# A list schedule with a price for the SBUF port of VectorE and GpSimd, in a kernel of attention and two feed-forward layers

## The chip, the cores and the metric

One core of a Trainium2 chip. The metric is the device time of one execution in microseconds, as a median of runs; the profile is of one execution.

## The reference

Attention for 2 batches x 8 heads x 768 positions x 64 dimensions, in which a query sees only keys of its own bucket (the signs of six projections), and then two feed-forward layers over 1536 tokens of width 512 with a hidden width of 2048:

```python
mask = q_bucket[:, :, :, None] == k_bucket[:, :, None, :]
scores = np.where(mask, scale * np.matmul(q, k.transpose(0, 1, 3, 2)), -1e9)
x = softmax(scores) @ v            # as (1536, 512)
h = np.maximum(x @ w_in, 0.0)
x = h * h @ w_out
h = x @ w2_in
out = (h * np.tanh(np.log1p(np.exp(h)))) @ w2_out
```

The four weight matrices come as 64-bit floats, which the kernel reads as pairs of 32-bit words and converts itself.

## The kernel before, in words

**Attention** (to about 224 us) is written out by hand in the order of its steps. Its last act on GpSimd (POOL) is `finish` (L564): it adds and scales the tiles `hi` and `rb` into `xf`, the input of the first layer. While it runs, five weight pieces are converted (`early`), so the feed-forward part begins with four up pieces and one down piece of its first group of weights.

**The feed-forward layers** go by a planner. Every 32-bit operand of a product is a pair of rounded parts, high and low; a product is three matmuls (`three`, L949 to L951): high x high, high x low, low x high. The hidden width of each layer is cut into four groups (`i` = 0 to 3 for the first layer, 4 to 7 for the second), each with 4 up pieces `wi` and 4 down pieces `wo`. The tokens form three blocks of 512. For each group the up products are:

- `classic`: block 0, four products of 12 matmuls (u = 0 to 7 in units of six matmuls);
- `seven`, twice: blocks 1 and 2 by seven half-size products in place of eight (Strassen's way), 6 matmuls each. They read sums of x blocks (`B11`, `B21`, `T1` to `T4`, `B22`, made once per layer by `blocks_x`) and sums of weights (`a`, `s`, made per group by `blocks_w`), and VectorE (DVE) puts the seven results together from PSUM (`add`, on DVE alone).

`activate` (L965) then takes relu and square, or mish, and splits the result into `gh` and `gl`. Down products (`half_down`, 24 per group, 6 matmuls each, numbered d) sum over the four pieces into four accumulators `acc` of PSUM; `collect` adds these to `tot`, by DVE (the first group of a layer is copied by ScalarE, ACT).

**The planner.** Each step is a `Task` with a due time, a cost for each engine that could do it, and what it comes after. `Plan.run` (L100) repeats: of all tasks whose inputs are planned, for each engine that would end it first, take the one that starts earliest, then the one due earliest; it is emitted on that engine's queue and the engine is taken to be busy for the cost. All engines work in order, so the plan is the order of their queues. It knows nothing of waits for memory that earlier tiles used. Its helpers:

- `both` (L765): a sum or difference of two tiles, on DVE or POOL; L770 is its instruction;
- `copy` (L774): a rounded copy, on ACT (L779) or POOL (L781);
- `parts`: a `copy` for the high part, a `both` for the low one;
- `convert` (L825): a load of a weight piece into one of two staging buffers, then on DVE magnitude (L842), bound (L845), move (L848), low (L851) and sign (L854), then `parts`;
- `when_up(u)` and `when_down(d)` give due times; `convert` and the x blocks are due some units before their products.

The table of activation functions for mish is loaded by a task of ACT at 100 of the plan's microseconds.

```python
    cost = {V: (n + 70) / 960, GP: 2.3e-3 * n + 0.12}       # both
    cost = {A: 0.833e-3 * n + 0.11, GP: 0.95e-3 * n + 0.2}  # copy
    plan.run({V: 2.5, A: 2.5, GP: 7.7, SP: 0.0, PE: 0.0})
```

Of the kernel before, what the change touches and what calls it, by code (L numbers as in the profile page):

```python
# [9 lines left out]
F32 = mybir.dt.float32  # L10
# [3 lines left out]
AF = mybir.ActivationFunctionType  # L14
ALU = mybir.AluOpType
# [4 lines left out]
EXP_SET, MISH_SET = TABLES.index("exp_and_others"), TABLES.index("mish")  # L20
# [17 lines left out]
class Buffer:  # L38


    def __init__(self, ring, size, make):
        self.ring, self.size, self.make = ring, size, make
        self.tile, self.left, self.end = None, 0, 0.0


class Task:

    def __init__(self, due, cost, emit, after, uses, lag):
        self.due, self.cost, self.emit, self.after, self.uses, self.lag = due, cost, emit, after, uses, lag
        self.end = self.behind = None  # L50


class Plan:
# [12 lines left out]
            self.rings.setdefault(ring, []).append(b)  # L66
        return b

    def task(self, due, cost, emit, after=(), uses=(), lag=0.0):
        t = Task(due, cost, emit, list(after), list(uses), lag)  # L70
        for b in t.uses:
            b.left += 1
        self.tasks.append(t)
        return t

    def given(self, end):
        t = Task(0.0, {}, None, [], [], 0.0)
        t.end = end
        return t

# [17 lines left out]
        return at  # L98

    def run(self, free):  # L100
        waiting = list(self.tasks)
        while waiting:
            best = {}
            for n, t in enumerate(waiting[:400]):
                at = self.ready(t)
                if at is None:
                    continue
                ends = {e: max(free[e], at) + c for e, c in t.cost.items()}
                first = min(ends.values())
                for e, c in t.cost.items():  # L110
                    if ends[e] <= first:
                        start = max(free[e], at)
                        key = (start, t.due, n)
                        if e not in best or key < best[e][0]:
                            best[e] = key, t
            e = min(best, key=lambda e: best[e][0])
            (start, _, _), t = best[e]
            for b in t.uses:
                if b.tile is None:
                    b.tile = b.make()  # L120
                    self.rings[b.ring].append(b)
            t.emit(e)
            free[e] = start + t.cost[e]
            t.end = free[e] + (t.lag or self.HOP)
            for b in t.uses:
                b.left -= 1
                b.end = max(b.end, t.end)
            waiting.remove(t)
# [3 lines left out]
def lsh_attention_relu2_mish_kernel(ctx, tc, qT, kT, vP, proj, w_in, w_out, w2_in, w2_out, out):  # L132
# [27 lines left out]
    def load_table(k):  # L160
        loaded.append(k)
        nc.scalar.add_instruction(
            mybir.InstLoadActFuncSet(act_func_set_id=k, name=nc.get_next_instruction_name(), ins=[], outs=[])
        )
# [581 lines left out]


    tmp = ctx.enter_context(tc.tile_pool(name="tmp", bufs=NTMP, reuse_waits="tile"))
    gp = ctx.enter_context(tc.tile_pool(name="gp", bufs=NGP, reuse_waits="tile"))
    wb = ctx.enter_context(tc.tile_pool(name="wb", bufs=1, reuse_waits="tile"))  # L750
    sw = ctx.enter_context(tc.tile_pool(name="sw", bufs=NS, reuse_waits="tile"))
    sf = ctx.enter_context(tc.tile_pool(name="sf", bufs=1, reuse_waits="tile"))
    pacc = ctx.enter_context(tc.tile_pool(name="pacc", bufs=4, reuse_waits="tile", space=PSUM))
    psh = ctx.enter_context(tc.tile_pool(name="psh", bufs=4, reuse_waits="tile", space=PSUM))
    wpools[1] = wb
# [8 lines left out]

    def both(due, out, a, b, n, after, uses, op=ALU.subtract, on=(V, GP)):  # L765

        cost = {V: (n + 70) / 960, GP: 2.3e-3 * n + 0.12}

        def emit(e):
            e.tensor_tensor(out(), a(), b(), op)  # L770

        return plan.task(due, {e: cost[e] for e in on}, emit, after, uses)

    def copy(due, out, a, n, after, uses, on=(A, GP), func=AF.Copy):  # L774
        cost = {A: 0.833e-3 * n + 0.11, GP: 0.95e-3 * n + 0.2}

        def emit(e):
            if e is A:
                e.activation(out(), a(), func)  # L779
            else:  # L780
                e.tensor_scalar(out(), a(), 1.0, 0.0, ALU.mult, ALU.add)  # L781

        return plan.task(due, {e: cost[e] for e in on}, emit, after, uses)

    def parts(due, high, low, a, n, after, uses):

# [5 lines left out]
    PERIOD, HALVES = 2 * FC + 2 * 7, 2 * FC * NBLK  # L792
    UNIT = 6 * 0.2265

    def when_up(u):
        return UNIT * (u + max(0.0, HALVES * (u - LAG) / PERIOD))

    def when_down(d):
        i, n = divmod(d, HALVES)
        u = LAG + PERIOD * d / HALVES  # L800
        if i == G - 1:
            u = min(u, G * PERIOD + 2 + 0.01 * n)
        return when_up(u) + (UNIT * n * 0.001)

    SA, SB = 2, 1
    ORDERS = {0: (0, 1, 2, 3), SB: (0, 1, 3, 2), SA: (0, 1, 2, 3)}
# [4 lines left out]


    W, Wd = {}, {}
    order = [None]

    def place(nm, i, f):
        W[nm, i, f] = plan.buffer("w" + nm, 5, lambda: new_place(nm, i, f))
# [7 lines left out]
    def convert(k, due):  # L825
        i, nm, src, f = pieces[k]
        if k in staged:
            s, load = plan.buffer("stg", 2, tile=staged.pop(k)), [plan.given(0.0)]
        else:
            s = tile_of(stg, [P, 512], I64, "stg", 2)  # L830
            load = [plan.task(due, {SP: 0.7}, lambda e: e.dma_start(out=s.tile, in_=src[i % G, :, f * 512:(f + 1) * 512]), [], [s], 4.5)]
        m = tile_of(stg, [P, 512], F32, "cv", 2)
        w = place(nm, i, f)

        def word(n):
            return s.tile.bitcast(U32).rearrange("p (n t) -> p n t", t=2)[:, :, n]

        def mu():
            return m.tile.bitcast(U32)

        def magnitude(e):
            e.tensor_scalar(mu(), word(1), 0x7FFFFFFF, None, ALU.bitwise_and)  # L842

        def bound(e):
            e.tensor_scalar(m.tile, m.tile, F64_LOW, F64_HIGH, ALU.max, ALU.min)  # L845

        def move(e):
            e.tensor_scalar(mu(), mu(), 3, 0x3FFFFFF8, ALU.logical_shift_left, ALU.bitwise_and)  # L848

        def low(e):  # L850
            e.scalar_tensor_tensor(mu(), word(0), 29, mu(), ALU.logical_shift_right, ALU.bitwise_or)  # L851

        def sign(e):
            e.scalar_tensor_tensor(mu(), word(1), 0xC0000000, mu(), ALU.bitwise_and, ALU.bitwise_or)  # L854

        after = load + [order[0]] * (order[0] is not None)
        for emit, cost in ((magnitude, 0.35), (bound, 0.35), (move, 0.35), (low, 0.61), (sign, 0.61)):
            after = [plan.task(due, {V: cost}, emit, after, [s, m])]
        order[0] = after[0]
        Wd[nm, i, f] = parts(due, lambda: w.tile[:, 0], lambda: w.tile[:, 1], lambda: m.tile, 512, after, [m, w])  # L860
        for t, prev in zip(Wd[nm, i, f][:1], last_w.get(nm, [])):
            t.after.append(prev)
        last_w[nm] = Wd[nm, i, f]

    last_w = {}
# [93 lines left out]
    def bank():  # L959
        return tile_of(psh, [P, TB], F32, "h", 4)  # L960

    ready, gb = {}, {}
    table = plan.task(100.0, {A: 2.0}, lambda e: load_table(MISH_SET), [plan.given(100.0)])

    def activate(i, blk, f, due, h, after, t=None):  # L965

        uses = [h] if t is None else []
        t = temporary() if t is None else t
        a = (lambda: t.tile) if not uses else (lambda: h.tile)
        o = copy(due, lambda: t.tile, a, TB, after + [table] * (i >= G), [t] + uses, (A,), AF.Relu if i < G else AF.Mish)  # L970
        due += 2
        if i < G:
            cost = {A: 0.54, V: 0.61, GP: 1.3}

            def square(e):
                if e is A:
                    e.activation(t.tile, t.tile, AF.Square)
                else:
                    e.tensor_tensor(t.tile, t.tile, t.tile, ALU.mult)

            o = plan.task(due, cost, square, [o], [t])
        if (i, blk, f) == (2 * G - 1, SA, FC - 1):
            gh, gl = (tile_of(tmp, [P, TB], F32R, "t", NTMP) for _ in range(2))
        else:
            gh, gl = (tile_of(gp, [P, TB], F32R, tag, NGP) for tag in ("gh", "gl"))
        gb[i, blk, f] = gh, gl
        r = copy(due, lambda: gh.tile, lambda: t.tile, TB, [o], [t, gh])
        ready[i, blk, f] = [r, both(due, lambda: gl.tile, lambda: t.tile, lambda: b32(gh.tile), TB, [r], [t, gh, gl])]
# [135 lines left out]
    for i in range(2 * G):  # L1124
        if i == G:
            X[1, "x"] = tile_of(act, [P, 2, PPB, TB], F32R, "xs", 1)
            for c in range(PPB):
                x_parts((1, "x"), c, when_up(G * PERIOD) - 4, lambda c=c: tot[0, 0].tile[:, c, :], [totd[0, c]], [tot[0, 0]])
            blocks_x(1, [tot[0, blk] for blk in range(NBLK)], dict(totd))
        if i:  # L1130
            for nm in "io":
# [60 lines left out]
```

## Time and profile before

| what | value |
|---|---|
| median of 3 runs | 777.0 us (775.19 to 779.73) |
| the profiled execution | 778.28 us, of which the span is 776.3 |
| TensorE (PE) busy | 739.3 us, 95% |
| VectorE (DVE) busy | 668.8 us, 86% |
| ScalarE (ACT) busy | 400.6 us, 52% |
| GpSimd (POOL) busy | 377.5 us, 49% |
| the chain that ended last | PE 55%, DVE 37%, issue 4%, ACT 2% |
| mean granted clock of TensorE | 0.98 |

Matmuls overlap, each one counted from its start to its end, so a TensorE that starts them at half its pace looks busy as well. The pace is read from the starts of neighbours, and the work of a stretch from its number of matmuls.

### The profile page before, as it was taken

The page shows a single profiled execution, that of the slowest core. Times are in us where ns is not written, and L with a number is a line of the kernel's source. Part 1 is how long each engine was busy: PE and PEld are TensorE (multiplying, and loading weights), DVE is VectorE, ACT ScalarE, POOL GpSimd, SP SyncE. Part 2 cuts the span into 40 slices and gives each one's busy share as a digit, 9 for nine tenths or more (in the row PEclk, how much of TensorE's full clock was granted, in tenths as well). Part 3 has the DMA queues.
Part 4 walks back from the last instruction along what each step waited for, and adds up shares of the span by engine and source line. Part 5 has one row for each costly group of instructions (what it writes and reads, how often), then busy time and mean ns, then how long its engine had stood idle before and what let it go on. Part 6 is the DMA issues. An engine that isn't in the chain of part 4 may idle for free.

```text
span 776.3 us, 10726 instructions
## 1 busy us (share of the span) xinstructions
PE 739.3 (95%) x3658; PEld 627.3 (81%) x3658; DVE 668.8 (86%) x1060; ACT 400.6 (52%) x729; POOL 377.5 (49%) x400
## 2 busy tenths in 40 slices
PE   8999999999996799899998998989999899999998
PEld 5999999999984488678887887867878688878887
DVE  8989998999959999999699799999989966995543
ACT  6989888988974354453343334434343322231320
POOL 8685967584228625145255136554644342561100
PEclk9999999999998899999999999998999999999999
DMA  6778777875310123221112121200222211120012
GB/s 183 210 187 215 185 170 203 214 176 133 97 51 0 30 79 109 84 97 64 56 54 82 54 79 58 82 28 27 82 82 81 82 55 54 55 77 4 1 55 108
DMA packets 29102, 72.70 MB, mean 94 GB/s; under 512 B 5064, under 2 KB 10536, under 8 KB 29048
## 3 DMA queue, kind: packets, MB, share of 16 engines
q1 hardware_dynamic: 28824, 71.88, 32.6%
q8 instruction: 29, 0.48, 0.3%
q14 instruction: 25, 0.20, 0.1%
q10 hardware_dynamic: 224, 0.13, 0.1%
HBM read 46.14 MB, written 3.19 MB: 64 GB/s over the span
## 4 chain that ended last, share of the span: by engine, by line
PE 55%; DVE 37%; issue 4%; ACT 2%; DMA 1%; POOL 1%; SPq 0%; POOLq 0%; ACTq 0%; DVEq 0%
PE acc L517 8%; PE s L462 8%; PE pT L488 8%; DVE t L770 7%; PE acc L949 6%; PE acc L951 6%; PE acc L950 6%; PE h L949 4%; PE h L951 4%; PE h L950 4%; DVE gl L770 4%; DVE a L770 3%; DVE cv L854 3%; DVE cv L851 3%; DVE cv L845 3%
## 5 line engine op out<-in xcount | busy, mean ns | idle before, releaser
L505 DVE TENSOR_TENSOR pl<-pT,ph 128x768 fp32r<-128x768 f32 x96 | 91.7, 956 | 16.7 <-ACT ph L501 10.5
L779 ACT ACTIVATE t<-t 128x512 f32<-128x512 f32 (+1 forms) x65 | 41.0, 632 | 119.6 <-DVE t L770 118.9
L478 ACT ACTIVATE e<-e,nm 128x768 f32<-128x768 f32 x96 | 89.8, 935 | 8.1 <-DVE e L469 7.9
L469 DVE TENSOR_SCALAR_CACHE_REDUCE e<-s 128x768 f32<-128x768 f32 x96 | 90.8, 946 | 0.9 <-PE s L462 0.8
L949 PE MATMUL acc<-gh,wo 128*128 128x512 f32 x192 | 76.6, 399 | 9.5 <-DVE tot L770 4.0
L501 ACT ACTIVATE ph<-pT 128x768 fp32r<-128x768 f32 x96 | 77.7, 809 | 12.2 <-PE pT L490 7.0
L770 DVE TENSOR_TENSOR t<-t,h 128x512 f32<-128x512 f32 x112 | 74.7, 678 | 9.5 <-PE h L951 9.5
L770 DVE TENSOR_TENSOR gl<-t,gh 128x512 fp32r<-128x512 f32 x79 | 62.0, 787 | 23.8 <-ACT gh L779 22.6
L488 PE MATMUL pT<-ident,e 128*128 128x128 f32 x576 | 78.9, 273 | 0.3 <-DVE e L469 0.2
L949 PE MATMUL acc<-wo,gh 128*128 128x512 f32 (+1 forms) x191 | 74.1, 388 | 5.0 <-DVE tot L770 5.0
L951 PE MATMUL acc<-gh,wo 128*128 128x512 f32 x192 | 75.8, 395 | 1.1 <-DVE wo L770 1.1
L950 PE MATMUL acc<-gl,wo 128*128 128x512 f32 x192 | 75.9, 395 | 0.0
L951 PE MATMUL acc<-wo,gl 128*128 128x512 f32 (+1 forms) x191 | 74.0, 388 | 0.6 <-DVE gl L770 0.6
L950 PE MATMUL acc<-wo,gh 128*128 128x512 f32 (+1 forms) x191 | 73.7, 386 | 0.0
L488 PEld LDWEIGHTS pT<-ident,e 128*128 128x128 f32 x576 | 67.4, 140 | 6.2 <-DVE e L469 1.6
L779 ACT ACTIVATE t<-h 128x512 f32<-128x512 f32 x48 | 28.4, 591 | 82.2 <-PE h L951 79.8
L770 POOL TENSOR_TENSOR a<-wi 128x256 f32<-128x256 f32 x44 | 41.3, 944 | 50.5 <-DVE wi L770 49.3
L770 DVE TENSOR_TENSOR tot<-tot,acc 128x512 f32<-128x512 f32 (+1 forms) x73 | 47.0, 674 | 19.0 <-PE acc L951 19.0
L770 POOL TENSOR_TENSOR s<-a,s 128x256 fp32r<-128x256 f32 x55 | 51.5, 947 | 2.8 <-ACT s L779 1.8
L949 PEld LDWEIGHTS acc<-gh,wo 128*128 128x128 f32 x192 | 36.7, 191 | 19.5 <-issue 8.2
L462 PE MATMUL s<-KA,QA 128*128 128x384 f32 x192 | 50.0, 342 | 0.4 <-DVE q_r L389 0.2
L462 PE MATMUL s<-KB,QB 128*128 128x384 f32 x192 | 49.3, 338 | 0.9 <-DVE QB L357 0.9
(191 smaller groups left out, 1926.4 us busy)
## 6 DMA issues: line engine op xcount, KB each, us to landing
stg<-in_w_in_dram SPq DMA_DIRECT2D x32, 512.0 KB
stg<-in_w_out_dram SPq DMA_DIRECT2D x32, 512.0 KB
KA<-kh SPq DMA_DIRECT2D x28, 192.0 KB
v_r<-in_vP_dram SPq DMA_DIRECT2D x8, 384.0 KB
rb<-rd SPq DMA_DIRECT2D x32, 96.0 KB
out_dram<-tot SPq DMA_DIRECT2D x11, 256.0 KB
q_r<-in_qT_dram SPq DMA_DIRECT2D x7, 384.0 KB
k_r<-in_kT_dram SPq DMA_DIRECT2D x7, 384.0 KB
```

Source lines behind the costliest of these rows:

```text
L462: nc.tensor.matmul(ps[:, o], a[:, q0:q0 + P], b[:, H2 * h:H2 * h + H2], start=n == 0, stop=n == 1)
L469: nc.vector.tensor_scalar(e.rearrange("p (h s) -> p h s", s=H2), x, MASKED, None, ALU.min, ALU.min, accum_out=nm)
L478: nc.scalar.activation(e, e, AF.Exp, bias=nm, scale=-1.0, accum_out=ssums[p, half][:, c:c + 1])
L488: nc.tensor.transpose(ps[:, c * P:(c + 1) * P], e[:, c * P:(c + 1) * P], ident)
L501: nc.scalar.activation(ph, v, AF.Copy)
L505: nc.vector.tensor_tensor(pl, v, b32(ph), ALU.subtract)
L517: nc.tensor.matmul(accs[g], w, phl[g][k // KT][:, c, :], start=k == 0, stop=k == 2 * KT - 1)
L770: e.tensor_tensor(out(), a(), b(), op)
L779: e.activation(out(), a(), func)
L949: PE.matmul(out, a[k][0], b[k][0], start=first and k == 0, stop=False)
L950: PE.matmul(out, a[k][0], b[k][1], start=False, stop=False)
L951: PE.matmul(out, a[k][1], b[k][0], start=False, stop=final and k == n - 1)
```

## The change

1. A task has a `port`: the engines on which it holds the SBUF port that DVE and POOL share. The planner starts such a task only when the port is free, and holds the port to its end. `both` holds it on either engine where POOL is a choice; the conversions' steps hold it on DVE, the square on DVE and POOL. Sums from PSUM, on DVE alone, don't. The costs of `both` and `copy` change a little.
2. `copy` is for ACT alone. The magnitude of a first-layer piece goes to ACT, as an activation (absolute value).
3. Due times: the first block's eight down products (d < 8) are due right behind the first four `classic` ones, and the up products from u = 8 on are put off by up to eight units; the rule for the last group of the first layer is written anew.
4. The table load comes behind the last magnitude and the first layer's last up product.
5. The pools `sw` and `sf` (tiles `s` and `a`) are allocated ahead of `gp` and `wb`. The magnitudes of successive pieces are no longer chained; the first step of a piece comes behind the high part of the piece before it.

```diff
+    def task(self, due, cost, emit, after=(), uses=(), lag=0.0, port=()):
...
     def run(self, free):
-        waiting = list(self.tasks)
+        waiting, port = list(self.tasks), 0.0
...
-                ends = {e: max(free[e], at) + c for e, c in t.cost.items()}
-                first = min(ends.values())
+                starts = {e: max(free[e], at, port if e in t.port else 0.0) for e in t.cost}
+                first = min(starts[e] + c for e, c in t.cost.items())
                 for e, c in t.cost.items():
-                    if ends[e] <= first:
-                        start = max(free[e], at)
-                        key = (start, t.due, n)
+                    if starts[e] + c <= first:
+                        key = (starts[e], t.due, n)
...
             free[e] = start + t.cost[e]
+            if e in t.port:
+                port = free[e]
...
     tmp = ctx.enter_context(tc.tile_pool(name="tmp", bufs=NTMP, reuse_waits="tile"))
+    sw = ctx.enter_context(tc.tile_pool(name="sw", bufs=NS, reuse_waits="tile"))
+    sf = ctx.enter_context(tc.tile_pool(name="sf", bufs=1, reuse_waits="tile"))
     gp = ctx.enter_context(tc.tile_pool(name="gp", bufs=NGP, reuse_waits="tile"))
     wb = ctx.enter_context(tc.tile_pool(name="wb", bufs=1, reuse_waits="tile"))
-    sw = ctx.enter_context(tc.tile_pool(name="sw", bufs=NS, reuse_waits="tile"))
-    sf = ctx.enter_context(tc.tile_pool(name="sf", bufs=1, reuse_waits="tile"))
...
-        cost = {V: (n + 70) / 960, GP: 2.3e-3 * n + 0.12}
+        cost = {V: (n + 66) / 960, GP: 2.5e-3 * n + 0.1}
...
-        return plan.task(due, {e: cost[e] for e in on}, emit, after, uses)
+        return plan.task(due, {e: cost[e] for e in on}, emit, after, uses, port=on if GP in on else ())
...
-    def copy(due, out, a, n, after, uses, on=(A, GP), func=AF.Copy):
-        cost = {A: 0.833e-3 * n + 0.11, GP: 0.95e-3 * n + 0.2}
+    def copy(due, out, a, n, after, uses, on=(A,), func=AF.Copy):
+        cost = {A: 0.833e-3 * n + 0.11, GP: 0.9e-3 * n + 0.2}
...
+    AHEAD = 8
+
     def when_up(u):
-        return UNIT * (u + max(0.0, HALVES * (u - LAG) / PERIOD))
+        return UNIT * (u + max(AHEAD * min(1.0, max(0.0, u - 7.5)), HALVES * (u - LAG) / PERIOD))
 
     def when_down(d):
-        i, n = divmod(d, HALVES)
-        u = LAG + PERIOD * d / HALVES
-        if i == G - 1:
-            u = min(u, G * PERIOD + 2 + 0.01 * n)
-        return when_up(u) + (UNIT * n * 0.001)
+        if d < AHEAD:
+            return UNIT * (8.01 + d)
+        if (G - 1) * HALVES <= d < G * HALVES:
+            return min(when_up(LAG + PERIOD * d / HALVES), when_up(G * PERIOD + 2) + 0.001 * d)
+        return when_up(LAG + PERIOD * d / HALVES)
...
         def magnitude(e):
-            e.tensor_scalar(mu(), word(1), 0x7FFFFFFF, None, ALU.bitwise_and)
+            if e is A:
+                e.activation(m.tile, s.tile.bitcast(F32).rearrange("p (n t) -> p n t", t=2)[:, :, 1], AF.Abs)
+            else:
+                e.tensor_scalar(mu(), word(1), 0x7FFFFFFF, None, ALU.bitwise_and)
...
-        after = load + [order[0]] * (order[0] is not None)
-        for emit, cost in ((magnitude, 0.35), (bound, 0.35), (move, 0.35), (low, 0.61), (sign, 0.61)):
-            after = [plan.task(due, {V: cost}, emit, after, [s, m])]
-        order[0] = after[0]
+        after = load + last_w.get(nm, [])[:1]
+        first = (A, 0.57) if i < G else (V, 0.35)
+        for emit, e, cost in ((magnitude, *first), (bound, V, 0.35), (move, V, 0.35), (low, V, 0.61), (sign, V, 0.61)):
+            after = [plan.task(due, {e: cost}, emit, after, [s, m], port=(V,))]
+            if e is A:
+                magnitudes.extend(after)
...
-        for t, prev in zip(Wd[nm, i, f][:1], last_w.get(nm, [])):
-            t.after.append(prev)
...
-    table = plan.task(100.0, {A: 2.0}, lambda e: load_table(MISH_SET), [plan.given(100.0)])
...
-            o = plan.task(due, cost, square, [o], [t])
+            o = plan.task(due, cost, square, [o], [t], port=(V, GP))
...
+            table.append(plan.task(when_up(G * PERIOD), {A: 1.4}, lambda e: load_table(MISH_SET), magnitudes + list(up[-1:])))
```

## Rows read from the trace of the kernel before

**Rows 1.** Windows by stage: us, each engine's busy us (instructions), TensorE's clock, DMA share, GB/s

```profile
224.60:300.00 75.40, 62.74 (x247) 48.25 (x246) 67.32 (x98) 35.11 (x66) 44.49 (x44) 0.91 0.17 50
300.00:515.00 215.00, 205.95 (x891) 169.04 (x891) 196.39 (x310) 89.38 (x154) 91.14 (x103) 0.98 0.21 69
515.00:540.00 25.00, 21.62 (x79) 15.68 (x78) 24.90 (x33) 11.50 (x21) 15.50 (x14) 0.86 0.12 40
540.00:700.00 160.00, 154.33 (x672) 126.70 (x671) 140.53 (x219) 51.39 (x92) 75.87 (x83) 0.99 0.22 70
...
224.60:776.30 551.70, 517.77 (x2217) 420.50 (x2215) 465.36 (x712) 202.45 (x356) 232.92 (x250) 0.97 0.19 62
```

**Rows 2.** Timeline of TensorE: neighbours at full pace, and behind a wait

```profile
244.07 0.63 PE L949 MATMUL h<-T,s 128*128 128x512 f32 x1
244.50 0.63 PE L950 MATMUL h<-T,s 128*128 128x512 f32 x1
...
406.72 0.39 PE L950 MATMUL h<-B,wi 128*128 128x512 f32 x1
406.95 0.39 PE L951 MATMUL h<-B,wi 128*128 128x512 f32 x1
```

**Rows 3.** Waits of TensorE from 224.6 us: in total, times, longest

```profile
PE acc L949 <- DVE tot L770: 9.0, 4, 3.2
PE h L950 <- DVE B L770: 5.7, 3, 3.1
PE h L950 <- DVE T L770: 4.2, 3, 3.3
```

**Rows 4.** Timeline of DVE beside an idle POOL: start us, duration us

```profile
258.60 0.68 DVE L854 SCALAR_TENSOR_TENSOR cv<-stg,cv 128x512 uint32<-128x512 uint32 x1
259.20 0.41 DVE L770 TENSOR_TENSOR a<-wi 128x256 f32<-128x256 f32 x1
259.54 0.42 DVE L842 TENSOR_SCALAR cv<-stg 128x512 uint32<-128x512 uint32 x1
259.88 1.21 DVE L770 TENSOR_TENSOR T<-t,T 128x512 fp32r<-128x512 f32 x1
```

**Rows 5.** Timelines of DVE and of POOL where both work

```profile
240.65 1.21 DVE L770 TENSOR_TENSOR gl<-t,gh 128x512 fp32r<-128x512 f32 x1
241.78 1.21 DVE L770 TENSOR_TENSOR B<-xf,B 128x512 fp32r<-128x512 f32 x1
...
241.27 1.17 POOL L770 TENSOR_TENSOR s<-a,s 128x256 fp32r<-128x256 f32 x1
```

**Rows 6.** L770 alone in the window; POOL's 256-wide groups of it (busy, mean ns, idle)

```profile
224.60:776.30 551.70, 295.01 (x410) 180.27 (x170) 0.97 0.19 62
...
L770 POOL TENSOR_TENSOR s<-a,s 128x256 fp32r<-128x256 f32 x55 | 51.5, 947 | 2.8 <-ACT s L779 1.8
L770 POOL TENSOR_TENSOR a<-wi 128x256 f32<-128x256 f32 x44 | 41.3, 944 | 50.5 <-DVE wi L770 49.3 <-DVE s L770 0.4
L770 POOL TENSOR_TENSOR a<-a,a 128x256 f32<-128x256 f32 x38 | 40.2, 1057 | 14.0 <-DVE a L770 13.2
```

**Rows 7.** Waits of DVE between 224.6 and 300 us

```profile
DVE a L770 <- POOL hi L568: 5.9, 1, 5.9
```

**Rows 8.** Timelines of ACT and TensorE at two losses; in brackets, idle before

```profile
322.84 0.63 ACT L779 ACTIVATE wo<-cv 128x512 fp32r<-128x512 f32 x1 [2.52 <-DVE cv L854]
...
325.44 0.47 PE L949 MATMUL acc<-gh,wo 128*128 128x512 f32 x1 [3.02 <-ACT tot L779]
...
416.13 0.47 PE L949 MATMUL acc<-gh,wo 128*128 128x512 f32 x1 [2.00 <-DVE tot L770]
```

**Rows 9.** Timeline of DVE at the boundary of the layers

```profile
516.12 5.32 DVE L770 TENSOR_TENSOR B<-tot,B 128x512 fp32r<-128x512 f32 x4
```

**Rows 10.** Timeline of ACT at the table load

```profile
347.94 1.28 ACT L162 ACT_TABLE_LOAD   x1
349.23 0.42 ACT L779 ACTIVATE s<-a 128x256 fp32r<-128x256 f32 x1
```

More of the change, by code (lines that the diff above doesn't have):

```diff
@@ L46, with __init__ @@
 class Task:
-    def __init__(self, due, cost, emit, after, uses, lag):
-        self.due, self.cost, self.emit, self.after, self.uses, self.lag = due, cost, emit, after, uses, lag
+    def __init__(self, due, cost, emit, after, uses, lag, port):
+        self.due, self.cost, self.emit, self.after, self.uses, self.lag, self.port = due, cost, emit, after, uses, lag, port
         self.end = self.behind = None
@@ L67, in buffer @@
         return b
-    def task(self, due, cost, emit, after=(), uses=(), lag=0.0):
-        t = Task(due, cost, emit, list(after), list(uses), lag)
+    def task(self, due, cost, emit, after=(), uses=(), lag=0.0, port=()):
+        t = Task(due, cost, emit, list(after), list(uses), lag, port)
         for b in t.uses:
@@ L76, in given @@
     def given(self, end):
-        t = Task(0.0, {}, None, [], [], 0.0)
+        t = Task(0.0, {}, None, [], [], 0.0, ())
         t.end = end
@@ L781, in emit @@
                 e.tensor_scalar(out(), a(), 1.0, 0.0, ALU.mult, ALU.add)
-        return plan.task(due, {e: cost[e] for e in on}, emit, after, uses)
+        return plan.task(due, {e: cost[e] for e in on}, emit, after, uses, port=(GP,))
     def parts(due, high, low, a, n, after, uses):
@@ L813, in lsh_attention_relu2_mish_kernel @@
     W, Wd = {}, {}
-    order = [None]
+    magnitudes = []
     def place(nm, i, f):
@@ L960, in bank @@
         return tile_of(psh, [P, TB], F32, "h", 4)
-    ready, gb = {}, {}
-    table = plan.task(100.0, {A: 2.0}, lambda e: load_table(MISH_SET), [plan.given(100.0)])
+    ready, gb, table = {}, {}, []
     def activate(i, blk, f, due, h, after, t=None):
@@ L969, in activate @@
         a = (lambda: t.tile) if not uses else (lambda: h.tile)
-        o = copy(due, lambda: t.tile, a, TB, after + [table] * (i >= G), [t] + uses, (A,), AF.Relu if i < G else AF.Mish)
+        o = copy(due, lambda: t.tile, a, TB, after + table, [t] + uses, (A,), AF.Relu if i < G else AF.Mish)
         due += 2
```

## The prediction

> **What bounds it now.** I read the windows by stage first. From 224.6 us on TensorE has one stream of products left: 2217 matmuls, 24 of them half as wide [rows 1]. At full clock one starts every 0.2265 us [rows 2], so they need 2193 x 0.2265 + 24 x 0.12 (my estimate for the half width) = 500 us. They take from 224.6 to 773, 548: some 48 us are lost, and nothing but these can be won. The same division, window by window, says where: 247 matmuls in 224.6 to 300 leave 19.5 us; 891 in 300 to 515 leave 13.2; 79 in 515 to 540 leave 7.1; 672 in 540 to 700 leave 7.8; behind 700 nothing is lost [rows 1]. The reader is to see VectorE (DVE) beside that: busy 88 to 99% of the windows where TensorE loses time, and 36 of the last 76 us, where it loses none.
>
> TensorE's waits name the same engine: DVE's `tot` adds, which free the accumulators, and the x blocks B and T [rows 3]. After a wait the clock adds to it: behind a wait for B that ends at 243.05, the longest with 3.1 us [rows 3], matmuls start every 0.43 us [rows 2], about the lower of the two levels (1.2 and 2.4 GHz), in a window with a mean granted clock of 0.91 [rows 1].
>
> Then why DVE is late. Beside an idle GpSimd (POOL) a 512-wide instruction with two SBUF inputs takes 0.60 us from start to start, a 256-wide one 0.34, a `tensor_scalar` 0.34 [rows 4]. Beside a busy POOL the 512-wide one takes 1.13, and POOL's 256-wide one 1.17 [rows 5], where the plan's price for it is 0.71 (its groups have means of 0.94 to 1.06 [rows 6]). The two hold each other up almost fully, and the plan before knows nothing of it: it prices each engine as if the other stood still.
>
> **The change, part by part.** *The port in the plan.* L770 issues 410 instructions on DVE and 170 on POOL; 137 of POOL's are 256 wide [rows 6]. At the prices of [rows 4] DVE's own 410 cost at most 410 x 0.60 = 246 us (some are narrower), the 59 pieces not converted early 59 x (3 x 0.34 + 2 x 0.60) = 131, the seven others of its 712 instructions 4: 381, where DVE was busy 465 [rows 1]. So POOL stretched DVE by 84 or more. If DVE did all of POOL's 170, that is 137 x 0.34 + 33 x 0.60 = 66. The magnitudes of the 27 pieces of the first layer that were not converted early leave DVE: minus 9. DVE then has 438 us against TensorE's 500, 88%, even if POOL does nothing. In the new plan POOL still wins a 256-wide task while DVE adds from PSUM, which takes no port there.
>
> *Rounded parts and magnitudes on ScalarE (ACT).* At most 80 POOL copies (250 instructions less the 170 [rows 1, 6]) and 27 magnitudes go to ACT at 0.63 [rows 8]: 67 us on an engine busy 202 of 552 [rows 1], so half used. Cover is there on average, but ACT works in order; the second rival prices that.
>
> *The table load* moves to the end of the first layer's last up product. It takes 1.28, and ACT's next instruction starts 1.29 after it [rows 10]. It then stands at the boundary, where x blocks wait for ACT's copies: 0 to 1.3 us, taken inside the boundary's term. The Trainium skill ("ScalarE: Activation LUTs", "What ACT_TABLE_LOAD costs") gives about 2.66 us for every switch, a drain behind the load included, which speaks against such a place; the trace shows no drain behind this one. By the page the sum would be 1.4 us longer.
>
> *Order of the pools.* DVE's first task of the plan, `a` from L770, waits 5.9 us for POOL's `hi` of the attention's tail [rows 7]: no data of it, so I read it as the memory of `sf` being that of `hi`. Moved below `gp` and `wb`, `sf` and `sw` lie elsewhere: gain 5.9 us of DVE, or none if the new place waits for another tile of the tail. I take the gain; the planner doesn't know of such waits.
>
> *First block's products due first.* Eight products (48 matmuls, 10.9 us) come behind the four `classic` ones. Three down weights are due earlier. SP has only loads left by then, so no queue is passed; the third load has to wait for a staging buffer. What becomes late is the x blocks, by 7.4 us of DVE; what covers it is the 10.9 us of products.
>
> **The sum.** *Start.* TensorE has 48 + 48 + 42 matmuls before the second group of seven: 31.3 us, to 255.9. DVE owes by then 4 low parts of activations (2.4), 3 conversions at 2 x 0.34 + 3 x 0.60 (7.4), 22 instructions of the x blocks (13.2), 12 of the first weight sums (4.1) and six adds (3.6): 30.7, from 225 on. That balances, with nothing over for hops to ACT; I leave one stall like that at 243 with its slow matmuls, 3.1 + 9 x 0.2 = 5 us. Bounds: 0, and 19.5 + 5.9 if earlier weights only push the x blocks back. *Middle* (21.0 now). It consists of seven losses (near 322, 348, 414, 479, 564, 615 and 682), most of them a wait for `tot` adds: 9.0 us in four [rows 3], as that of 2.0 before 416 [rows 8]. Per group of weights DVE owes about 51 us (8 conversions 20, 12 low parts 7, 26 adds 16, 24 half-wide sums 8) to TensorE's 62.5. The plan's clock for DVE then holds, so adds come when the plan has them; I take 1 us for each of the seven: 7. Bounds 0 and 21, or more by the second rival. *Boundary* (7.1 now). Four B parts took 5.32 us beside POOL [rows 9], 2.4 alone; 22 x-block instructions need 13.2, while TensorE has 10.9 of `classic` and more if the next down products are ready. I take 3, bounds 1 and 8.4 (7.1 and the load). Lost: 15 in place of 47.6, a gain of 32.6. The profiled execution (778.28, span 776.3) would come to 745.7; against the median of 777.0 that is **744 us**.
>
> On the lock: by [rows 5] one POOL sum costs a DVE instruction beside it 1.13 - 0.60 = 0.53, and DVE does it in 0.34. The Trainium skill ("SBUF — State Buffer", "Who interferes with whom") says that the one fully blocks, with no sharing. By that a pair would take 0.60 + 0.71 = 1.31 where the trace has 1.13 to 1.17; the change would then give DVE twice as much (0.37 a pair, not 0.19), and the start's 5 us might go as well: 739.
>
> **The rivals.** *First: only one half comes.* (a) The start stays bound by DVE, because the wait of [rows 7] moves to another tile or the weights push the x blocks out: 744 + 14.5 = 759. For it: [rows 1] has DVE at 67 of 75 us there, and my balance has nothing over. (b) The start comes, but the middle's waits remain, since POOL works less there (91 of 215 us, to 44 of 75 at the start) and DVE is full all the same [rows 1]: 777 - 14.5 = 762. Against: 51 of 62.5 us per group leave DVE room to catch up.
>
> *Second: ACT becomes the late engine, and it is slower.* Its place is the in-order queue of ACT. At 322.84 a rounded weight waited 2.5 us there for DVE's conversion, the copies of `tot` stood behind it, and TensorE lost 3.0 [rows 8], 4.9 with the slow matmuls behind. The change adds 107 such entries, and the magnitude puts an ACT step at the head of each conversion. It decides from 32.6 / 4.9 = seven such stalls beyond those I left; with ten the time is 744 + 49 = 793. Against: ACT is half idle, and the plan prices ACT right.
>
> *Third: no change*, where the total work of DVE, not its stretch, holds TensorE: 777, give or take 4. Against: 438 of 500, and 465 now.
>
> **How the numbers follow.** Forecast 0.55 (its own range 733 to 755: the middle's 7 us and 4 more gone, or the load and two more stalls like that at 243), rival 1a 0.12, 1b 0.15, third 0.07, second 0.11. The range reaches to 1a and 1b and 5 us past them: 733 to 767; the third and second, 0.18, lie outside. A measurement here tells 0.5% (4 us) from no change. Faster 0.82, same 0.07, slower 0.11.
>
> **What would show it.** Right: POOL under 80 us behind 224.6, without copies of L781; DVE's 512-wide low parts near 0.68 us each, as the conversions' steps of [rows 4]; no wait for `hi` at DVE's first task; eight `acc` products before the first T product; a granted clock over 0.97 in the first window. Wrong: DVE's first task waits for another tile; ACT's queue ahead of TensorE's waits; seven or more waits over 2 us behind 300.

## The result, and the profile after

The changed kernel takes 734.34 us (734.06 to 734.59), the one before 777.51 on the same chip: a ratio of 0.9445, 95% interval 0.9416 to 0.9474. That is 43 us less, where 33 were forecast.

In the changed kernel the sums of `both` stand at L772, ACT's copies at L781 and the three matmuls of a product at L956 to L958; in the other kernels these lines shift by a few. The windows by stage, as in [rows 1] (the one from 700 us on left out):

```profile
224.60:300.00 75.40, 72.87 (x313) 57.62 (x312) 73.20 (x139) 54.13 (x104) 24.71 (x14) 1.00 0.21 71
300.00:515.00 215.00, 215.00 (x950) 178.05 (x949) 190.66 (x346) 120.52 (x216) 35.94 (x34) 1.00 0.19 67
515.00:540.00 25.00, 25.00 (x112) 20.70 (x111) 23.79 (x52) 12.14 (x24) 1.79 (x2) 1.00 0.24 85
540.00:700.00 160.00, 160.00 (x707) 132.49 (x706) 129.74 (x237) 62.07 (x111) 17.98 (x18) 1.00 0.16 56
...
224.60:733.00 508.40, 502.47 (x2218) 413.67 (x2216) 431.37 (x792) 252.66 (x458) 80.42 (x68) 1.00 0.19 67
```

Divide again as the prediction did. 950 matmuls at 0.2265 us fill all of the 215 us from 300 to 515; the next two windows are full as well; the first lacks 75.4 - 313 x 0.2265 = 4.5 us, where it lacked 19.5. So all of the 43 us came out of TensorE's lost time, which went from some 48 us to about 5, and what is left lies before 264 us. The granted clock of these windows is 1.00 throughout, where it was 0.91, 0.98, 0.86 and 0.99. DVE does 792 instructions in place of 712 and is busy 34 us less; POOL went from 233 us to 80, ACT's busy time from 202 to 253.

TensorE's waits behind 224.6 us are short now, 2.3 us in all (in total, times, longest); of [rows 3] only T is left:

```profile
PE h L958 <- DVE s L772: 0.8, 2, 0.5
PE h L956 <- ACT s L781: 0.7, 1, 0.7
PE h L957 <- DVE T L772: 0.6, 1, 0.6
PE acc L958 <- DVE wo L772: 0.2, 1, 0.2
```

POOL keeps 63 sums of 170, nearly all 256 wide. The groups (busy, mean ns, idle before and its releasers), as in [rows 6], have means no better than before: where POOL still works, it works beside DVE.

```profile
L772 POOL TENSOR_TENSOR s<-a,s 128x256 fp32r<-128x256 f32 x26 | 33.4, 1290 | 203.8 <-ACT s L781 165.8 <-DVE t L772 36.7 <-DVE a L772 1.2
L772 POOL TENSOR_TENSOR a<-wi 128x256 f32<-128x256 f32 x18 | 20.2, 1123 | 66.3 <-DVE wi L772 65.5 <-DVE s L772 0.4
L772 POOL TENSOR_TENSOR a<-a,a 128x256 f32<-128x256 f32 x14 | 14.8, 1060 | 40.6 <-DVE a L772 29.9 <-PE h L958 10.5
```

DVE's 512-wide low parts `gl`, before and after:

```profile
L770 DVE TENSOR_TENSOR gl<-t,gh 128x512 fp32r<-128x512 f32 x79 | 62.0, 787 | 23.8 <-ACT gh L779 22.6 <-POOL gh L781 1.2
L772 DVE TENSOR_TENSOR gl<-t,gh 128x512 fp32r<-128x512 f32 x94 | 66.9, 725 | 29.8 <-ACT gh L781 29.7
```

### The profile page after: what moved, and what is told of

Its sections match the earlier page's. It is cut to its first block, busy times and chain, and to the rows that moved or that the text cites. A ratio compares the mean times of both kernels' runs of the same rounds, so it can differ in the third digit from the quotient of the medians.

```text
span 732.8 us, 10720 instructions
## 1 busy us (share of the span) xinstructions
PE 723.9 (99%) x3658; PEld 620.5 (85%) x3658; DVE 634.8 (87%) x1140; ACT 450.9 (62%) x831; POOL 224.8 (31%) x218
## 4 chain that ended last, share of the span: by engine, by line
PE 91%; DVE 5%; DMA 1%; issue 1%; POOL 1%; ACT 1%; SPq 0%; POOLq 0%; ACTq 0%; DVEq 0%
PE acc L956 11%; PE acc L958 11%; PE acc L957 11%; PE h L958 10%; PE h L956 10%; PE h L957 10%; PE s L464 9%; PE acc L519 9%; PE pT L490 8%; PE bits L383 1%; DVE t L772 1%; DVE e L471 1%; DVE T L772 1%; POOL xf L575 0%; DMA w<-in_proj_dram 0%
## 5 line engine op out<-in xcount | busy, mean ns | idle before, releaser
L772 POOL TENSOR_TENSOR s<-a,s 128x256 fp32r<-128x256 f32 x26 | 33.4, 1290 | 203.8 <-ACT s L781 165.8
L772 DVE TENSOR_TENSOR gl<-t,gh 128x512 fp32r<-128x512 f32 x94 | 66.9, 725 | 29.8 <-ACT gh L781 29.7
L781 ACT ACTIVATE t<-t 128x512 f32<-128x512 f32 (+1 forms) x65 | 40.9, 631 | 79.9 <-DVE t L772 79.8
L772 DVE TENSOR_TENSOR t<-t,h 128x512 f32<-128x512 f32 x112 | 75.1, 683 | 15.5 <-PE h L958 14.9
L781 ACT ACTIVATE t<-h 128x512 f32<-128x512 f32 x48 | 28.6, 595 | 76.3 <-PE h L958 76.1
L958 PE MATMUL acc<-gh,wo 128*128 128x512 f32 x192 | 74.8, 390 | 0.2 <-DVE wo L772 0.2
L956 PE MATMUL acc<-gh,wo 128*128 128x512 f32 x192 | 74.8, 390 | 0.0
L958 PE MATMUL acc<-wo,gl 128*128 128x512 f32 (+1 forms) x191 | 73.7, 386 | 0.0
L956 PE MATMUL acc<-wo,gh 128*128 128x512 f32 (+1 forms) x191 | 73.7, 386 | 0.0
L772 DVE TENSOR_TENSOR tot<-tot,acc 128x512 f32<-128x512 f32 (+1 forms) x73 | 47.0, 676 | 19.6 <-PE acc L958 19.6
L781 ACT ACTIVATE gh<-t 128x512 fp32r<-128x512 f32 x95 | 58.0, 626 | 1.4
L957 PE MATMUL h<-xs,wi 128*128 128x512 f32 x128 | 49.8, 389 | 0.0
```

Of the source, the lines that this page charges most:

```text
L956: PE.matmul(out, a[k][0], b[k][0], start=first and k == 0, stop=False)
L957: PE.matmul(out, a[k][0], b[k][1], start=False, stop=False)
L958: PE.matmul(out, a[k][1], b[k][0], start=False, stop=final and k == n - 1)
```

## The experiments

Twelve kernels, e1 to e12: five undo one part of the change, four put one part, or what it amounts to, into the kernel before, one takes POOL out of the sums, and two measure the port by itself. Each ratio is to the kernel before, measured beside it on the same chip; between chips that kernel had medians of 777.5 to 778.9 us, so small differences are read from the ratios. Theory A: POOL's work beside DVE stretches DVE, and pricing the port is the main piece. Theory B: the copies on ScalarE, or the due times, are.

**Undoing the port (e1).**

```diff
-            if e in t.port:
-                port = free[e]
```

> The changed kernel, whose planner no longer holds the port (it is always free); all else stays. Theory A (the price of the port is the main piece): the plan gives POOL sums as if it were free again, POOL is busy over 120 us behind 224.6 instead of 80, DVE's 512-wide low parts go from 0.73 back to about 0.79, waits for tot adds come back in the middle, and 15 to 30 us of the 43 are lost: 750 to 765 us. Theory B (the copies on ScalarE, the due times and the pools do it): 734 to 740 us.

Measured: 759.59 us, ratio 0.976 (0.9742 to 0.9777). The window that lost nothing loses again, and TensorE's waits are back:

```profile
224.60:300.00 75.40, 63.93 (x266) 50.26 (x265) 69.90 (x102) 44.62 (x86) 48.14 (x39) 0.95 0.17 57
300.00:515.00 215.00, 207.57 (x903) 169.86 (x902) 188.61 (x303) 115.14 (x206) 65.29 (x61) 0.99 0.18 67
```

```profile
PE acc L954 <- ACT wo L779: 6.7, 1, 6.7
PE acc L954 <- DVE tot L770: 5.5, 4, 1.8
PE h L954 <- DVE t L770: 3.2, 1, 3.2
```

75.4 - 266 x 0.2265 = 15.2 us are lost at the start and 215 - 903 x 0.2265 = 10.5 in the second window. POOL works 165 us behind 224.6. Theory A holds; 25 of the 43 us hang on two lines of a planner. The longest wait now names ACT: a rounded weight, for which ACT itself stood 4.9 us until DVE's conversion of it was done. That is the second rival's mechanism, and here it starts with a late DVE.

**Copies on POOL again (e2)**, with the port held there.

```diff
-    def copy(due, out, a, n, after, uses, on=(A,), func=AF.Copy):
+    def copy(due, out, a, n, after, uses, on=(A, GP), func=AF.Copy):
```

> The changed kernel, in which rounded copies may go to POOL again, priced 0.9 ns an element + 0.2 and holding the port there. Theory A: the planner seldom gives POOL a copy, since it ends later there and has to wait for the port; 734 to 738 us. Theory B (ScalarE alone for copies is the main piece): 750 us or more.

Measured: 736.84 us, ratio 0.9466 (0.9447 to 0.9486), which the interval of the changed kernel takes in. The planner gave POOL 40 copies, 32 us of work, not the few that were expected. With the port priced, the copies' place is worth some 2 us by the medians, and the runs don't tell that from nothing.

**Sums on DVE alone (e3).**

```diff
-    def both(due, out, a, b, n, after, uses, op=ALU.subtract, on=(V, GP)):
+    def both(due, out, a, b, n, after, uses, op=ALU.subtract, on=(V,)):
```

> The changed kernel with every sum on DVE alone (no POOL in the feed-forward part, except squares if the planner wants one there). Theory A (POOL is worth little beside DVE, DVE alone suffices at 88% of TensorE's time): 733 to 738 us, DVE free of stretch at 0.68 for a 512-wide low part. Rival C (the 63 sums that POOL still does in DVE's PSUM adds carry the balance): the start loses 5 to 15 us more, 740 to 750 us.

Measured: 736.36 us, ratio 0.9463 (0.9443 to 0.9482), not told apart from the changed kernel. DVE is busy 441 us, and its low parts `gl` have a mean of 687 ns where the changed kernel has 725 and the one before 787 (the window from 224.6 us on, and the group of DVE: busy, mean, idle):

```profile
224.60:736.00 511.40, 504.20 (x2218) 414.97 (x2216) 441.14 (x856) 253.66 (x455) 8.48 (x7) 1.00 0.18 67
...
L772 DVE TENSOR_TENSOR gl<-t,gh 128x512 fp32r<-128x512 f32 x95 | 64.1, 687 | 27.1 <-ACT gh L781 27.0
```

POOL's 63 sums are worth nothing that these times can measure, though the first window, with 298 matmuls, loses 7.9 us in place of 4.5.

**The pools in the old order (e4)** (`sw` and `sf` behind `wb` again).

> The changed kernel with the pools sw and sf allocated last again. Theory A (memory of hi below sf): DVE's first sum of weights waits about 5.9 us for POOL's hi, DVE is the late engine of the start, and 5 to 8 us with slow matmuls come back: 739 to 743 us. Rival D (the start has slack once the port is priced): the wait is there but hidden, 734 to 736 us.

Measured: 738.14 us, ratio 0.9483 (0.9466 to 0.9499), just under the 739 expected, and without slow matmuls: the first window has a granted clock of 1.00. DVE's waits up to 300 us, as in [rows 7]; in the changed kernel none of these two is there:

```profile
DVE a L772 <- DMA rb<-rd: 5.9, 1, 5.9
DVE a L772 <- POOL xf L575: 1.3, 1, 1.3
```

The tile `a` shares no data with the attention's tail, and only the order of the pools differs, so the wait is one for memory. Whose memory stays open: the same 5.9 us are put down to `hi` in the kernel before [rows 7] and to the load of `rb` here; `finish` works on both. The first window has 296 matmuls, a loss of 8.4 us: of the 7.2 that DVE stands, TensorE pays 3.9.

**The port alone, in the kernel before (e5)**: the planner's lines and the new costs of sums; copies may use POOL.

> The kernel before with the port and the new costs of sums in the planner, and nothing else of the change: copies may still go to POOL (holding the port there), magnitudes on DVE, old due times, old pools, old place of the table load. Theory A (the price of the port is the main piece): the waits in the middle go, those of the start go in part, because DVE's first task still waits for hi and the x blocks come ahead of products; 742 to 752 us. Theory B: 760 us or more.

Measured: 743.61 us, ratio 0.9557 (0.953 to 0.9583).

**No POOL, in the kernel before (e6)**: both `on=(V,)` and `on=(A,)`, no port in the planner.

> The kernel before with sums on DVE alone and rounded copies on ScalarE alone, no port in the planner, all else as before. Theory A in its narrow form (what counts is that POOL no longer works beside DVE, however that is brought about): as good as the port alone, 742 to 752 us. Rival E (the planner has to know the port, and DVE with all sums is too full, 447 of 500 us with magnitudes): 755 us or more.

Measured: 743.80 us, ratio 0.9558 (0.9532 to 0.9585). The first two windows, of the port alone and then without POOL:

```profile
224.60:300.00 75.40, 67.20 (x272) 53.33 (x272) 68.14 (x132) 42.03 (x80) 27.56 (x20) 0.93 0.18 60
300.00:515.00 215.00, 215.00 (x950) 178.07 (x950) 200.18 (x371) 104.57 (x183) 52.76 (x49) 1.00 0.19 68
```

```profile
224.60:300.00 75.40, 66.54 (x269) 51.11 (x268) 66.79 (x140) 43.92 (x85) 4.22 (x5) 0.95 0.17 58
300.00:515.00 215.00, 215.00 (x950) 178.11 (x949) 201.54 (x396) 113.13 (x200) 0.00 (x0) 1.00 0.19 68
```

These two are the sharpest pair. They come to the same time by different plans, and in both the middle loses nothing although DVE is busy 200 of 215 us. What the port's price does is to leave POOL less to do beside DVE (127 us in e5, where it was 233); a planner without a word of ports does as well once it has no POOL. That the copies on ScalarE, which e6 has too, are not enough for it shows in e12 below: there POOL keeps its sums, and to take these away as well makes 743.80 of 768.40. What both leave is the start: 13.8 and 14.5 us lost.

**The old due times (e7)** in the changed kernel (`when_up` and `when_down` as before).

> The changed kernel with the old due times of up and down products. If the first block's products due first cover the making of the x blocks: TensorE waits at the first B and T products again, 4 to 10 us of the start come back, 738 to 745 us. If the planner would run them there anyway, as ready before the x blocks: 733 to 736 us.

Measured: 739.36 us, ratio 0.9502 (0.9475 to 0.9529). TensorE loses 75.4 - 287 x 0.2265 = 10.4 us at the start, at a granted clock of 0.95, with waits that are back at the T products (T is an x block, `s` a sum of weights):

```profile
PE h L954 <- ACT T L781: 1.8, 1, 1.8
PE h L956 <- DVE s L772: 1.0, 1, 1.0
PE h L955 <- DVE T L772: 0.9, 2, 0.6
```

**Magnitudes on DVE (e8).**

```diff
-        first = (A, 0.57) if i < G else (V, 0.35)
+        first = (V, 0.35)
```

> The changed kernel with all magnitudes on DVE. 27 x 0.34 = 9 us go back to DVE over the first layer, where it is fullest. If DVE has no slack in the start: 2 to 4 us more there, 736 to 738 us. If it has, or if the step on ScalarE costs as much: 733 to 735 us.

Measured: 735.71 us, ratio 0.9455 (0.9424 to 0.9486): between the two ranges expected, and nothing that can be told from the changed kernel.

**The due times and the pools alone, in the kernel before (e11).**

> The kernel before with the new due times and the new order of the pools, and nothing else. Theory A (these two mend the start alone, and only where DVE isn't stretched): 4 to 12 us faster than before, 766 to 774 us; the middle's waits for tot stay. If they did more by themselves: 760 us or less.

Measured: 776.17 us, ratio 0.9961 (0.9947 to 0.9974): 3 us, under the 4 to 12 expected. These two, whose undoing costs 8 us or so by the ratios of e4 and e7, give 3 without the port. The first window still loses 16 us (262 matmuls), and TensorE's waits are much as in the kernel before:

```profile
PE acc L951 <- DVE tot L770: 9.3, 4, 3.5
PE acc L953 <- DVE wo L770: 4.7, 2, 2.7
PE acc L951 <- ACT tot L779: 4.1, 1, 4.1
```

**The copies on ScalarE alone, in the kernel before (e12).**

> The kernel before with rounded copies on ScalarE alone, and nothing else. Theory A: POOL loses 49 us of copies but takes more sums, since the planner finds it free; DVE stays stretched; 765 to 778 us. Theory B (copies are a main piece): 755 us or less.

Measured: 768.40 us, ratio 0.9868 (0.9851 to 0.9885). A fall of 10 us. POOL loses its 49 us of copies and takes 155 sums, where more than its 170 were expected; DVE is busy 12 us less with 16 instructions more, so POOL's copies seem to have held DVE up as well (no run takes them away and leaves the sums as they were). POOL still works 170 us, and TensorE still waits:

```profile
224.60:767.10 542.50, 512.56 (x2219) 420.00 (x2217) 453.23 (x728) 237.94 (x432) 170.55 (x160) 0.97 0.20 63
```

**The port by itself (e9).** The kernel with sums on DVE alone (squares not on POOL either) gets one idle stream on POOL, on a tile of its own:

```diff
+    du = dum.tile([P, 256], F32, tag="du", name="du")
+    nc.gpsimd.memset(du, 1.0)
+    for _ in range(140):
+        nc.gpsimd.tensor_tensor(du, du, du, ALU.mult)
```

> The changed kernel with all sums on DVE and all squares on DVE or ScalarE, and 140 idle 256-wide multiplications on POOL, of one tile of its own that nobody else touches, queued when the feed-forward part begins. They share no data with anything. Theory A (the port is held by either): POOL needs about 1.15 us for each beside DVE, DVE's 512-wide instructions go to 1.13 us from start to start for some 160 us, DVE falls behind by 55 to 75 us, 785 to 810 us against 736 without them. Rival F (DVE was stretched by waits for data, not by the port): 734 to 740 us.

Measured: 780.37 us, ratio 1.0021 (1.001 to 1.0032): all of the gain is gone, with work that shares not one datum with the rest. It is less than the 785 to 810 expected: the stream lasts 127 us and not 160, and costs DVE 0.42 us an instruction where [rows 5] had 0.53. The stream, with the shortest, median and longest multiplication in ns, and the timeline of DVE beside it (start, duration):

```profile
L759 POOL TENSOR_TENSOR du<-du x140: 612/897/1122, 234.4 to 360.3; 128x256 f32<-128x256 f32 x140
...
300.87 1.10 DVE L990 TENSOR_TENSOR t<-t 128x512 f32<-128x512 f32 x1
301.88 1.09 DVE L777 TENSOR_TENSOR wi<-cv,wi 128x512 fp32r<-128x512 f32 x1
302.90 0.83 DVE L857 TENSOR_SCALAR cv<-cv 128x512 f32<-128x512 f32 x1
303.65 0.83 DVE L777 TENSOR_TENSOR a<-wi 128x256 f32<-128x256 f32 x1
304.41 0.83 DVE L860 TENSOR_SCALAR cv<-cv 128x512 uint32<-128x512 uint32 x1
```

512-wide instructions start 1.02 us apart in place of 0.60, 256-wide ones and the `tensor_scalar` 0.76 in place of 0.34 [rows 4]: each loses 0.42, whatever its length. The groups of DVE from 236 to 350 us show which kinds pay:

```profile
L777 DVE TENSOR_TENSOR gl<-t,gh 128x512 fp32r<-128x512 f32 x16 | 15.7, 992 | 0.0
L777 DVE TENSOR_TENSOR t<-t,h 128x512 f32<-128x512 f32 x16 | 10.7, 674 | 0.0
```

The low parts take 992 ns in the mean; the sums `t<-t,h`, which read one operand from PSUM, take 674, as in the kernel without the stream (683 in e3). The change leaves these without a port, and rightly.

**Fills in place of the reads (e10).** The same with 420 fills (`memset` of the tile) in place of the multiplications:

> The same with 420 fills (no reading of SBUF) of that tile in place of the multiplications. If only POOL's reading holds DVE up: DVE's low parts stay at 0.68 to 0.70, 735 to 738 us. If writing holds the port as well: DVE stretched for as long as the fills last, 750 us or more.

Measured: 735.40 us, ratio 0.944 (0.9426 to 0.9454). POOL is busy 140 us with them, and DVE's timeline is at its own pace:

```profile
240.40 0.68 DVE L777 TENSOR_TENSOR B<-xf,B 128x512 fp32r<-128x512 f32 x1
241.00 0.68 DVE L777 TENSOR_TENSOR gl<-t,gh 128x512 fp32r<-128x512 f32 x1
241.60 0.68 DVE L777 TENSOR_TENSOR wo<-cv,wo 128x512 fp32r<-128x512 f32 x1
```

The groups from 236 to 370 us, with the fills and, for comparison, in e3 without them:

```profile
L777 DVE TENSOR_TENSOR gl<-t,gh 128x512 fp32r<-128x512 f32 x28 | 18.8, 681 | 5.8 <-ACT gh L786 5.8
L857 DVE TENSOR_SCALAR cv<-cv 128x512 f32<-128x512 f32 x19 | 9.3, 490 | 0.1
...
L772 DVE TENSOR_TENSOR gl<-t,gh 128x512 fp32r<-128x512 f32 x27 | 18.2, 686 | 6.6 <-ACT gh L781 6.6
L852 DVE TENSOR_SCALAR cv<-cv 128x512 f32<-128x512 f32 x19 | 8.0, 422 | 0.0
```

The kernels of e9 and e10 differ in POOL's idle instructions alone, and they lie 45 us apart, as does DVE's busy time behind 224.6 (488 and 442 us). So POOL's multiplications, which read SBUF, hold up DVE's instructions with two SBUF inputs, and `tensor_scalar`; fills, which only write it, don't hold up the former, and `tensor_scalar` by 0.07 us. An instruction of POOL that reads without computing was not run.

## Why the prediction came out as it did

- **Where time was lost, and that nothing else could be won** (48 us of TensorE behind 224.6): right. 43 of them were won, and TensorE's part up to 224.6 is as it was. The measured 734.34 lies 10 us below the forecast, at the lower edge of the range.
- **DVE stretched by POOL, and able to do all sums itself**: right, and shown by e6 against e12, by e3, and by e9 against e10. The sum counted 438 us for all sums on DVE, at most; e3 has 441. Two signs were missed by a little: POOL works 80.4 us, not under 80, and the low parts take 725 ns, not 680. That POOL would win its sums while DVE adds from PSUM came out in part at best: its 256-wide groups still take 1060 to 1290 ns in the mean, so most of those sums meet DVE's reads. What the change brought is that there are fewer of them.
- **Start, 5 us left**: measured 4.5, and that the two agree is in part luck. The 5 were one long stall with slow matmuls behind it; what came are five short waits, none over 0.7 us, at a granted clock of 1.00. Both gains are there: the old due times cost 5.9 us of the first window (e7), the old pools 3.9 (e4). That DVE's debt would just about equal TensorE's work is borne out: DVE is busy 45.0 of the 45.4 us from 224.6 to 270. Six down products, not eight, came before the first T product: the planner put the two B products between.
- **Middle, 7 us left**: this is the term that was mis-sized; measured 0. I left 1 us for each of seven waits, from no row. In e5 and e6 DVE carries 200 of 215 us there and TensorE loses nothing. That the plan's order is the real order once DVE keeps its own prices would explain it; no run shows that by itself.
- **Boundary, 3 us left**: mis-sized too; measured 0. In the changed kernel the second layer's up products begin at 462.73, and its x blocks are made while TensorE has down products of the first layer, which lie between the up products; before, 48 matmuls of up products stood in a row, from 512.38 to 530.73, and TensorE waited for B and T among them. The port alone does as well: e5 loses nothing from 300 to 700 us.
- **Table load**: it stands where the step put it, behind the first layer's last up product, but no x block waits for ACT there and TensorE goes on at full pace. The up products run so far ahead that the first layer's down products fill the gap, and ACT's copies for the x blocks come only at 474.92. TensorE's timeline, then ACT's:

```profile
461.15 0.39 PE L958 MATMUL h<-T,wi 128*128 128x512 f32 x1
461.37 0.39 PE L956 MATMUL acc<-gh,wo 128*128 128x512 f32 x1
...
462.73 0.39 PE L956 MATMUL h<-xs,wi 128*128 128x512 f32 x1
...
462.55 1.28 ACT L164 ACT_TABLE_LOAD   x1
463.84 0.63 ACT L781 ACTIVATE t<-t 128x512 f32<-128x512 f32 x1
...
474.92 1.23 ACT L781 ACTIVATE B<-tot 128x512 fp32r<-128x512 f32 x2 [3.22 <-DVE tot L772]
```

  The next activation starts 1.29 us after it, as before [rows 10]. The Trainium skill ("ScalarE: Activation LUTs", "What ACT_TABLE_LOAD costs") gives 2.66 us with a drain; neither trace has one.
- **Order of the pools**: right in that it is the order which makes the wait, and that the planner can't see it: it cost DVE 5.9 us and, for `xf`, 1.3 more. That it is the memory of `hi` is not shown (e4).
- **ACT as the late engine**: did not come. ACT took 50 us more; TensorE's one wait for it is 0.7 us.
- **The lock**: the Trainium skill ("SBUF — State Buffer", "Who interferes with whom") has two-input instructions of DVE wait for a GpSimd instruction that reads SBUF, not for one that only writes, and those with one SBUF input outside the two-port modes not at all. The last three readings, 992, 681 (the mean of `gl` beside fills, 686 without, both from 236 to 370 us) and 674 ns, agree. Whether the one fully blocks the other, for the whole of its instruction, these runs don't settle: the shortest multiplication took 0.61 us, and each DVE instruction in the timeline lost 0.42.

With the 10 us of middle and boundary taken off, the forecast would have been 734.

## What to carry to other kernels

Before work is handed to GpSimd, see whether VectorE's instructions have the same start-to-start time beside it; if they don't, a part of GpSimd's busy time is taken from VectorE (here 0.42 to 0.53 us for each sum, which VectorE does itself in 0.34), and a plan that counts GpSimd as a second engine is wrong by as much. Here all of GpSimd's sums could go with no loss that the times show. And the first wait of an engine in a new stage is worth a look: a tile that shares no data with what it waits for may have taken over its memory, and here another order of allocation took the wait away.

## What was not expected of the hardware

The loss of a DVE instruction beside POOL's 256-wide multiplication was a fixed 0.42 us for a 256-wide and a 512-wide one alike (in the timeline of e9), so the narrow ones more than double and the wide ones take 70% longer. Beside fills, `tensor_scalar` alone was a little slower: 490 ns in the mean (bound, L857), against 422 without them (groups from 236 to 370 us). Beside the changed kernel's DVE, POOL's `s<-a,s` took 1290 ns in the mean where the plan prices 0.74 us: the plan's two engines are not held apart on the chip, they meet less often.
